# Decode attention at the end of the V stream: a second step multiplied in turned form

## The chip, the cores and the metric

The kernel runs on one core of one Trainium2 chip. The metric is device time in microseconds, some 1.7 us more than the span from the first to the last instruction that a profile shows; runs are quoted as medians with their range.

Engines: PE is the matrix engine (PEld its weight loads), DVE the vector engine, ACT the scalar engine, POOL the general one, SP the queue that issues the big loads. The *granted clock* is the share of PE's full clock that the profile shows as granted, 1.0 or 0.5. A transfer's *landing* is the moment at which the profile shows it complete. The *tail* is what happens from the last softmax to the end.

## The reference

One token attends to a cache of 65536 keys; 16 query heads share 8 heads of K and V, 256 wide. A small token mixer is added through a gate. Only the attention matters here:

```python
Hq, Hkv, Sk, Dh = 16, 8, 65536, 256
scores = einsum("bhqd,bhkd->bhqk", q, k) * (Dh ** -0.5)
p = softmax(scores, axis=-1)
o = einsum("bhqk,bhkd->bhqd", p, v)          # sum over 65536 keys
a = o.reshape(B, Sq, Hq * Dh) @ wo
...                                          # b: the mixer, small
return g * a + (1 - g) * b
```

K and V together are 537 MB in bf16 (2 x 8 x 65536 x 256 x 2 bytes), and each byte is read once. The kernel is a stream.

## The kernel before

Each head's keys are cut into chunks of 5 or 6 steps of 16 key blocks (128 keys each). A chunk's K and V each land in one slot of a ring of three. For every step DVE turns K (`turn`), and PE multiplies it with the queries (`scores`). After the chunk, ACT takes exponentials, DVE turns them (`pT`), and `p_v` multiplies V with them, eight matmuls for a step.

`p_v` keeps the probabilities as weights and streams 512 columns of V through PE. Its result has rows that must be summed and turned onto partitions: `pv` is copied to SBUF (`pvs`), and `o_turn` multiplies it with selector columns, in fp32, into `o_ps`. The *turned form*, `p_v_turned`, does it the other way about: V is the weights, the probabilities are two columns, and the result is added to `o_ps` directly. It takes 32 matmuls of 2 columns for a step in place of 8 of 512, and needs neither copy nor `o_turn`. The kernel before uses it for the very last step alone, which comes as two pieces of 12 and 4 key blocks.

```python
TAIL = 4

def load(item):
    ...
    elif item == 2 * total - 1:              # the last chunk: K and V in pieces
        for s in range(last):
            piece(item - 1, s * SB, SB)      # K, 1 MB each
        for s in range(last - 1):
            piece(item, s * SB, SB)          # V steps 0 to 3, 1 MB each
        piece(item, (last - 1) * SB, SB - TAIL)   # V step 4: 768 KB
        piece(item, last * SB - TAIL, TAIL)       # V step 4: 256 KB

def p_v(i, s):
    ...
    for k in range(SB // 2):
        ...
        nc.tensor.matmul(
            pv[g % 2][32 * a:32 * a + 4, :], lhsT=pT[:, k, :, s], rhs=vt[:, j * DH:(j + 2) * DH], ...)

def o_turn(g):                               # 4 fp32 matmuls (8 in the trace): pvs -> o_ps
    ...
def p_v_turned(i, s, lo, hi):
    ...
    for j in range(lo, hi):
        for c in range(2):
            at = (s * SB + j) * DH + c * 128
            nc.tensor.matmul(
                o_ps[:, 2 * c:2 * c + 2], lhsT=vt[:, at:at + 128], rhs=pT[:, j, :, s], ...)

...                                          # in the loop over chunks, at the end of a chunk:
    for s in range(sizes[c] - (i == total - 1)):
        p_v(i, s)
...                                          # after the loop:
nc.vector.tensor_copy(out=pvs[:, 0:DH], in_=pv[g % 2][:, 0:DH])
nc.scalar.activation(out=pvs[:, DH:2 * DH], in_=pv[g % 2][:, DH:2 * DH], func=ACT.Copy)
o_turn(g)
p_v_turned(i, s, 0, SB - TAIL)
p_v_turned(i, s, SB - TAIL, SB)
...                                          # scale (oT), output projection (acc), bias (res), store
```

The softmax here doesn't subtract the row's maximum and nothing guards it: scores larger than these inputs give would overflow.

## Time and profile before

| | before |
|---|---|
| time | 1273.73 us (1273.19 to 1273.82, 3 runs) |
| span of the profiled run | 1272.2 us |
| busy: PE / DVE / ACT | 57% / 49% / 5% |
| HBM read | 428 GB/s over the span |

The first view is the page's part in 40 slices. DMA is the busy share of the 16 DMA engines in tenths.

```profile
DMA  9999999999999999999999999999999999999997
GB/s 408 426 428 433 432 439 429 429 432 433 435 432 431 431 433 435 431 432 431 432 438 429 432 433 437 435 425 435 431 435 436 427 432 435 436 438 425 432 429 301
```

The stream is full from start to end. The Trainium skill, "DMA: Bandwidth & Descriptors", section "Where 436 GB/s comes from", gives a fabric ceiling of 435 GB/s; all but the first and the last of this trace's slices lie at it (425 to 439). The same section has a lower limit, about 358 GB/s, bind for loads from HBM; this trace of one core read 428, so here the measurement decides. So only what happens after the stream has run dry can be shortened by a change of PE's work. That is the last slice, and the next view shows it: the timeline of the last 10 us. Columns are start, duration, engine, line, operation, result and operands, count, and in brackets the idle time of the engine just before and what ended it.

```profile
1262.25 2.73 PE L382 MATMUL pv<-ring,pT 128*4 128x512 bf16 x24
...
1265.25 0.81 PE L382 MATMUL pv<-ring,pT 128*4 128x512 bf16 x8 [0.26 <-DMA ring<-in_A_v_cache_dram]
...
1266.11 0.42 DVE L472 COPY pvs<-pv 128x256 f32<-128x256 f32 x1 [3.32 <-PE pv L382]
...
1266.59 1.05 PE L414 MATMUL misc<-sel,pvs 128*128 128x2 f32 x8 [0.54 <-DVE pvs L472]
...
1267.51 0.97 PE L425 MATMUL misc<-pT,ring 128*128 128x2 bf16 x32
```

The order: 24 `p_v` for steps 0 to 2, a wait for step 3's V piece, 8 `p_v` for it, the copy, `o_turn` (L414), 32 turned matmuls (L425). The chain of waits names the same things as the ones that decided the end (start, duration, what):

```profile
1245.05 20.16 DMA ring<-in_A_v_cache_dram
1265.20 0.04 issue
1265.25 0.84 PE pv L382 x8
1266.09 0.02 issue
1266.11 0.44 DVE pvs L472
1266.55 0.04 issue
1266.59 1.05 PE misc L414 x8
1267.64 0.84 PE misc L425 x32
```

Two more numbers are needed: when the last pieces land. The view of DMA issues over a window gives the time from issue to landing, in its last column. This is the 256 KB piece, issued at 1249.86:

```profile
ring<-in_A_v_cache_dram SPq DMA_DIRECT2D x1, 256.0 KB, 17.8
```

It lands at 1249.86 + 17.8 = 1267.66. The 768 KB piece lands at 1247.51 + 19.5 = 1267.0. (Landing times are printed to a tenth, so these sums are good to 0.05 us, and a difference of two of them to 0.1.) The last turned matmul ends at 1268.49, which is 0.83 us after the last byte is there.

### The profile page before, as it was taken

The page shows a single profiled execution, that of the slowest core. Times are in us where ns is not written, and L with a number is a line of the kernel's source. Part 1 is how long each engine was busy: PE and PEld are TensorE (multiplying, and loading weights), DVE is VectorE, ACT ScalarE, POOL GpSimd, SP SyncE. Part 2 cuts the span into 40 slices and gives each one's busy share as a digit, 9 for nine tenths or more (in the row PEclk, how much of TensorE's full clock was granted, in tenths as well). Part 3 has the DMA queues.
Part 4 walks back from the last instruction along what each step waited for, and adds up shares of the span by engine and source line. Part 5 has one row for each costly group of instructions (what it writes and reads, how often), then busy time and mean ns, then how long its engine had stood idle before and what let it go on. Part 6 is the DMA issues. An engine that isn't in the chain of part 4 may idle for free.

```text
span 1272.2 us, 10454 instructions
## 1 busy us (share of the span) xinstructions
PE 723.6 (57%) x4552; PEld 285.1 (22%) x4552; DVE 626.8 (49%) x388; ACT 58.4 (5%) x149; POOL 78.5 (6%) x145
## 2 busy tenths in 40 slices
PE   1566556654666546564565646655465555665467
PEld 1222122221222112221222212222122212222123
DVE  2555354644555355453554445544455435544455
ACT  0000000000000000000000000000000000000000
POOL 4110101111011110110000000000000000000000
PEclk9978777888788877888778888888788887878778
DMA  9999999999999999999999999999999999999997
GB/s 408 426 428 433 432 439 429 429 432 433 435 432 431 431 433 435 431 432 431 432 438 429 432 433 437 435 425 435 431 435 436 427 432 435 436 438 425 432 429 301
DMA packets 16842, 544.90 MB, mean 428 GB/s; under 512 B 2202, under 2 KB 2332, under 8 KB 3484
## 3 DMA queue, kind: packets, MB, share of 16 engines
q1 hardware_dynamic: 15416, 540.55, 98.5%
q0 software_dynamic: 1376, 3.69, 0.8%
q8 instruction: 35, 0.57, 0.2%
q14 instruction: 11, 0.09, 0.0%
q10 hardware_dynamic: 4, 0.00, 0.0%
HBM read 544.22 MB, written 0.00 MB: 428 GB/s over the span
## 4 chain that ended last, share of the span: by engine, by line
DMA 63%; PE 17%; DVE 11%; issue 8%; ACT 1%; POOL 0%; DVEq 0%; ACTq 0%; SPq 0%; POOLq 0%
DMA ring<-in_A_k_cache_dram 59%; PE sc L359 12%; DVE kT L351 9%; PE pv L382 5%; DMA zb<-in_B_b_dram 2%; DMA ring<-in_A_v_cache_dram 2%; DVE pT L370 1%; ACT p L366 1%; PE den_ps L398 0%; PE misc L270 0%; DVEq L351 0%; PE acc L314 0%; PE misc L414 0%; PE misc L274 0%; PE misc L425 0%
## 5 line engine op out<-in xcount | busy, mean ns | idle before, releaser
L359 PE MATMUL sc<-kT,qw 128*128 128x512 bf16 x2048 | 575.7, 434 | 443.8 <-DVE kT L351 442.8
L351 DVE STREAM_TRANSPOSE kT<-ring 128x2048 f32<-128x2048 f32 x256 | 575.3, 2288 | 478.1 <-DMA ring<-in_A_k_cache_dram 396.1
L359 PEld LDWEIGHTS <-qw 128*128 128x128 bf16 x2048 | 215.5, 108 | 791.5 <-DVE kT L351 332.2
L382 PE MATMUL pv<-ring,pT 128*4 128x512 bf16 x2040 | 125.7, 395 | 62.1 <-DVE pT L370 61.8
L370 DVE STREAM_TRANSPOSE pT<-p 128x512 bf16<-128x512 bf16 x48 | 34.2, 712 | 130.9 <-ACT p L366 130.9
L382 PEld LDWEIGHTS <-pT 128*4 128x4 bf16 x2040 | 46.6, 89 | 135.0 <-DVE pT L370 81.7
L366 ACT ACTIVATE p<-sc 128x512 bf16<-128x512 f32 x48 | 28.7, 597 | 1037.6 <-PE sc L359 1037.6
L143 POOL DMA_DIRECT2D wo<-in_A_wo_dram x8 | 6.3, 790 | 549.7 <-PE acc L314 549.7
L333 POOL TENSOR_SCALAR t_b<-t_b 128x448 f32<-128x448 f32 x14 | 7.9, 564 | 224.8 <-ACT t_b L325 224.5
L336 POOL TENSOR_TENSOR t_b<-t_b,u_b 128x448 f32<-128x448 f32 x14 | 16.0, 1142 | 1.2
L343 POOL TENSOR_TENSOR gel<-t_b,u_b 128x448 bf16<-128x448 f32 x14 | 15.9, 1133 | 1.2
L339 POOL TENSOR_SCALAR t_b<-t_b,half_g 128x448 f32<-128x448 f32 x14 | 8.9, 636 | 106.9 <-ACT t_b L338 101.9
L414 PEld LDWEIGHTS misc<-sel,pvs 128*128 128x128 f32 x64 | 11.8, 258 | 3.7 <-issue 2.0
L398 PE MATMUL den_ps<-pick,dsum 128*128 128x2 f32 x32 | 4.8, 256 | 12.5 <-DVE dsum L390 12.5
L227 PE MATMUL misc<-zb,one_f 1*128 1x2 f32 x2 | 0.5, 342 | 19.7 <-DMA zb<-in_B_b_dram 19.7
L325 ACT ACTIVATE t_b<-h_bc,b1T,w1T 128x448 f32<-128x448 f32 x14 | 10.5, 751 | 4.7 <-DVE h_bc L257 4.7
L414 PE MATMUL misc<-sel,pvs 128*128 128x2 f32 x64 | 10.2, 281 | 0.5 <-DVE pvs L472 0.5
L329 POOL TENSOR_SCALAR u_b<-h_bc,w1T,b1T 128x448 f32<-128x448 f32 x14 | 10.0, 716 | 2.1 <-DVE qT L277 0.9
L230 DVE TENSOR_SCALAR gate<-gate 128x2 f32<-128x2 f32 x1 | 0.2, 169 | 18.9 <-ACT gate L229 18.9
L366 ACT ACTIVATION_READ_ACCUMULATOR p<-sc 128x1 f32 x48 | 9.3, 194 | 0.0
L164 POOL TENSOR_SCALAR_AFFINE_SELECT pick<-pick 128x2 f32<-128x2 f32 x44 | 8.6, 197 | 3.0 <-POOL pick L164 0.2
L338 ACT ACTIVATE t_b<-t_b 128x448 f32<-128x448 f32 x14 | 8.0, 572 | 13.4 <-POOL t_b L336 13.4
(75 smaller groups left out, 66.0 us busy)
## 6 DMA issues: line engine op xcount, KB each, us to landing
ring<-in_A_k_cache_dram SPq DMA_DIRECT2D x31, 5120.0 KB, 29.8
ring<-in_A_v_cache_dram SPq DMA_DIRECT2D x31, 5120.0 KB, 23.4
ring<-in_A_k_cache_dram SPq DMA_DIRECT2D x16, 6144.0 KB, 33.0
ring<-in_A_v_cache_dram SPq DMA_DIRECT2D x16, 6144.0 KB, 28.0
ring<-in_A_k_cache_dram SPq DMA_DIRECT2D x5, 1024.0 KB, 25.1
ring<-in_A_v_cache_dram SPq DMA_DIRECT2D x4, 1024.0 KB, 22.6
wo<-in_A_wo_dram POOLq DMA_DIRECT2D x8, 448.0 KB, 19.5
ring<-in_A_wq_dram SPq DMA_DIRECT2D x1, 3072.0 KB, 10.1
```

The costliest lines, as they stand in the source:

```text
L164: nc.gpsimd.affine_select(out=t, in_=t, compare_op=ALU.not_equal, fill=1.0, base=-row, pattern=[[step, w]], channel_multiplier=1,)
L325: nc.scalar.activation(out=t_b[:], in_=h_bc[:], func=ACT.Square, scale=w1T[:, b:b + 1], bias=b1T[:, b:b + 1],)
L329: nc.gpsimd.tensor_scalar(out=u_b[:], in0=h_bc[:], scalar1=w1T[:, b:b + 1], scalar2=b1T[:, b:b + 1], op0=ALU.mult, op1=ALU.add,)
L336: nc.gpsimd.tensor_tensor(out=t_b[:], in0=t_b[:], in1=u_b[:], op=ALU.mult)
L339: nc.gpsimd.tensor_scalar(out=t_b[:], in0=t_b[:], scalar1=1.0, scalar2=half_g[:, 0:1], op0=ALU.add, op1=ALU.mult,)
L343: nc.gpsimd.tensor_tensor(out=gel[:], in0=t_b[:], in1=u_b[:], op=ALU.mult)
L351: nc.vector.transpose(out=kT[n % 2][:].bitcast(FP32), in_=kn[:, s * SB * 128:(s + 1) * SB * 128])
L359: nc.tensor.matmul(sc[i % 2][:], lhsT=qw[g % 2][:, q, PAD - s:PAD - s + 128], rhs=kv[:, :, q // 2, :, q % 2], start=(s == 0 and q == 0), s ...
L366: nc.scalar.activation(out=p_t[i % 2][:], in_=sc[i % 2][:], func=ACT.Exp, scale=scale, accum_out=den[g % 2][:, c:c + 1],)
L370: nc.vector.transpose(out=pT_t[i % 2][:], in_=p_t[i % 2][:])
L382: nc.tensor.matmul(pv[g % 2][32 * a:32 * a + 4, :], lhsT=pT[:, k, :, s], rhs=vt[:, j * DH:(j + 2) * DH], start=first and k < 4, stop=last ...
L414: nc.tensor.matmul(o_ps[:, 2 * c:2 * c + 2], lhsT=pvs[:, lo:lo + 128], rhs=sel[:, 2 * half:2 * half + 2], start=(half == 0 and c == 0), st ...
```

## The change

Step 3 is taken from `p_v` and multiplied in turned form too. The intent: the sums of steps 0 to 2 are copied and turned while step 3's V is still on its way, so that after the landing only turned matmuls are left.

```diff
-        last = (g, c, s) == (HKV - 1, n_chunks - 1, sizes[c] - 2)
+        last = (g, c, s) == (HKV - 1, n_chunks - 1, sizes[c] - 3)
@@ p_v_turned
-                    start=False, stop=(j == SB - 1 and c == 1), skip_group_check=True,
+                    start=False, stop=(s == sizes[-1] - 1 and j == SB - 1 and c == 1), skip_group_check=True,
@@ end of a chunk
-        for s in range(sizes[c] - (i == total - 1)):
+        for s in range(sizes[c] - 2 * (i == total - 1)):
             p_v(i, s)
@@ after the loop
     o_turn(g)
+    p_v_turned(i, s - 1, 0, SB)
     p_v_turned(i, s, 0, SB - TAIL)
     p_v_turned(i, s, SB - TAIL, SB)
```

On PE, 8 matmuls of 512 columns go out and 32 of 2 columns come in, after `o_turn` instead of ahead of it. No other engine's order changes.

## The prediction

> **What bounds the kernel.** The stream of K and V out of HBM. The page's DMA row is 9 in 39 of 40 slices, 428 GB/s over the span of 1272.2 us; PE is busy 57%, DVE 49%. The Trainium skill, "DMA: Bandwidth & Descriptors", section "Where 436 GB/s comes from", puts the fabric ceiling at 435 GB/s; this trace's slices (408 to 439 GB/s) sit at it. The change leaves it alone: only the last part of PE's instructions differs. So only the tail counts.
>
> **The tail before** (timeline and chain of waits, us from the span's start). K's last turn ends at 1258.2, scores at 1260.2, softmax and its transpose at 1261.6, den at 1262.25. Then 24 matmuls of p_v for steps 0 to 2 take 2.73 us, without a wait for a DMA, to 1264.98; PE's granted clock is 0.5 from about 1262.3 to 1265.7. Step 3 is waited for 0.26 us: its V piece (issued 1245.05, 20.16 us to landing) lands at 1265.21. The chain from there: 8 matmuls of p_v 0.84, copy of pv 0.44, o_turn 1.05 (weights of the next group start 0.81 after its start), 32 turned matmuls to 1268.49, oT 0.17, acc 0.40, res 0.33, store. The last two pieces (768 and 256 KB) land at 1267.0 and 1267.66, from issue time plus time to landing.
>
> **What changes.** Removed: 8 matmuls of p_v (0.84 us) and the wait (0.26 us) ahead of the copy; copy and o_turn start 1.1 us earlier, at about 1265.0 and 1265.5. Added: 32 turned matmuls; 32 took 0.97 us, 30 ns each, so +0.97 us. These lie on the critical path too, because PE becomes free at about 1266.4, when step 3 has long landed: 64 turned matmuls need 1.94 us, to about 1268.35. Gain: 1.11 - 0.97 = 0.14 us. The floor is the last piece: 1267.66 plus 8 matmuls (0.25 us) and drain, about 1268.0; so 0.5 us is the most that could be gained without moving the stream.
>
> Against it: o_turn now begins at 1265.5, where the clock was still 0.5; 0.2 us or more of it could run at half speed and eat the gain. The Trainium skill, "TensorE: Matmul & The Clock Gate", section "What's actually happening", says that the clock is judged over free-running windows of 3.4 us; the trace agrees (0.5 for 3.4 us). Their phase may differ from run to run.
>
> So PE's work is exchanged nearly one for one. Effect -0.1 us, plausibly -0.5 to +0.6; runs of before differ by 0.6 us.
>
> **Predicted time:** 1273.6 us, 8 in 10 within 1272.2 to 1274.9. Faster by over 2%: 0.5%; within 2%: 99%; slower: 0.5%.
>
> **What would show it.** The timeline: the copy of pv starts before or at the landing of step 3's piece (about 1265.0); o_turn no longer follows a DMA wait; 64 turned matmuls in one run, 1.9 to 2.0 us; end of the last turned matmul to end of span as before (about 3.7 us). In the chain, p_v for the last step's 8 matmuls is gone, and the DMA link ends either at an earlier K piece (the chain then passes through scores, softmax and 24 p_v matmuls) or at one of the last two V pieces.
>
> **What would make it wrong.** A stream that is faster or slower by 0.1% (1.3 us) on this build or chip, which would hide everything. The turned matmuls running at half clock (60 ns each: +2 us). The last pieces landing later.

## The result

| | median us | range | runs |
|---|---|---|---|
| before | 1273.78 | 1273.19 to 1274.00 | 4 |
| after | 1274.62 | 1273.23 to 1275.34 | 4 |
| ratio | 1.0006 | 95%: 0.9989 to 1.0023 | |

Ratios are those on record; they are not quite the ratios of the medians that I quote. The verdict is "same". The profiled run of the changed kernel has a span of 1271.5 us. Its timeline at the end:

```profile
1261.82 1.47 PE L382 MATMUL pv<-ring,pT 128*4 128x512 bf16 x24
...
1263.35 0.42 DVE L472 COPY pvs<-pv 128x256 f32<-128x256 f32 x1 [0.98 <-PE pv L382]
...
1263.83 1.05 PE L414 MATMUL misc<-sel,pvs 128*128 128x2 f32 x8 [0.53 <-DVE pvs L472]
...
1264.75 0.98 PE L425 MATMUL misc<-pT,ring 128*128 128x2 bf16 x32
...
1266.58 0.98 PE L425 MATMUL misc<-pT,ring 128*128 128x2 bf16 x32 [0.85 <-DMA ring<-in_A_v_cache_dram]
```

and its chain of waits:

```profile
1247.59 18.93 DMA ring<-in_A_v_cache_dram
1266.53 0.05 issue
1266.58 0.99 PE misc L425 x32
1267.57 0.02 issue
1267.59 0.17 DVE oT L478
```

The 256 KB piece was issued at 1249.96 in this run:

```profile
ring<-in_A_v_cache_dram SPq DMA_DIRECT2D x1, 256.0 KB, 17.2
```

Three things differ from before. Step 3's `p_v` has left the chain. `p_v` of the other steps took 1.47 us, not 2.73, because the granted clock was 1.0 here and 0.5 in the profile of before. And PE now *waits* 0.85 us, with everything else done, for the 768 KB piece of step 4. The last turned matmul ends at 1267.57, which is 0.41 us after the last landing (1249.96 + 17.2 = 1267.16), where before it was 0.83.

So this one pair of traces would say "0.4 us gained" (0.83 against 0.41), while the runs say "0.8 us lost". Both are below the 0.1% by which single runs differ, and the two traces were not at the same clock. The two profiled runs were also the slowest of the four of before (1274.00) and the fastest of the four of the changed kernel (1273.23). The experiments sort this out.

### The profile page after: what moved, and what is told of

The parts are those of the page before. It is cut to its first block, busy times and chain, and to the rows that moved or that the text cites. A ratio compares the mean times of both kernels' runs of the same rounds, so it can differ in the third digit from the quotient of the medians. Undisturbed runs are those within 1.5% of the kernel's fastest.

```text
span 1271.5 us, 10502 instructions
## 1 busy us (share of the span) xinstructions
PE 740.7 (58%) x4576; PEld 291.7 (23%) x4576; DVE 627.8 (49%) x388; ACT 58.4 (5%) x149; POOL 78.4 (6%) x145
## 4 chain that ended last, share of the span: by engine, by line
DMA 62%; PE 19%; DVE 11%; issue 6%; ACT 1%; POOL 0%; DVEq 0%; ACTq 0%; SPq 0%; POOLq 0%
DMA ring<-in_A_k_cache_dram 59%; PE sc L359 14%; DVE kT L351 9%; PE pv L382 5%; DMA zb<-in_B_b_dram 2%; DMA ring<-in_A_v_cache_dram 1%; DVE pT L370 1%; ACT p L366 1%; PE den_ps L398 0%; PE misc L270 0%; PE acc L314 0%; DVEq L351 0%; PE misc L425 0%; PE misc L274 0%; DVE dsum L390 0%
## 5 line engine op out<-in xcount | busy, mean ns | idle before, releaser
L359 PE MATMUL sc<-kT,qw 128*128 128x512 bf16 x2048 | 587.8, 441 | 425.6 <-DVE kT L351 424.3
L359 PEld LDWEIGHTS <-qw 128*128 128x128 bf16 x2048 | 218.9, 109 | 780.9 <-DVE kT L351 324.0
## 6 DMA issues: line engine op xcount, KB each, us to landing
wo<-in_A_wo_dram POOLq DMA_DIRECT2D x8, 448.0 KB, 18.8
```

What stands on the lines that cost most here:

```text
L359: nc.tensor.matmul(sc[i % 2][:], lhsT=qw[g % 2][:, q, PAD - s:PAD - s + 128], rhs=kv[:, :, q // 2, :, q % 2], start=(s == 0 and q == 0), s ...
```

## The experiments

Two theories at first. **A**: the change shortens the tail by a few tenths, by filling a wait with work, and that is lost in the scatter of the stream. **B**: the change itself costs the 0.06%. As a rival inside A stood the reckoning of the prediction: PE's own chain of work decides, and the exchange 0.84 for 0.97 us settles the gain.

### Both kernels again

No edit. Both were run for five rounds beside common runs of the kernel before.

> The kernel before, unchanged, as the ruler: what two equal kernels differ by. Theory A (the change is worth 0.1 to 0.4 us in the tail, whole runs differ by more): ratio to before 1.000 with single runs spread over 0.5 to 2 us. Tail in the profile: from the landing of the last V piece to the last turned matmul 0.5 to 0.9 us, depending on whether p_v of the tail falls into a half-clock window. Theory B (the change itself costs 0.06%, 0.8 us): this run shows 1.0000 and the run of the changed kernel beside it shows 1.0006 again.

> The changed kernel, unchanged, a second time beside the ruler. Theory A: ratio within 0.999 to 1.001 and not distinguishable from the ruler; in the profile the last turned matmul ends about 0.4 us after the last V piece lands if the clock is full, and up to 0.9 us if p_v runs at half clock (then 64 turned matmuls in one run, no wait). Theory B: 1.0006 again, that is 0.8 us slower, with a later landing of the last V piece.

Measured: the kernel before again 1273.75 us (1273.50 to 1274.22, 5 runs), ratio 1.0000, interval 0.9987 to 1.0012. The changed kernel again 1273.68 us (1273.29 to 1275.07, 5 runs), ratio 1.0001, interval 0.9988 to 1.0015. The shared runs of before were 1273.92 us (1273.23 to 1274.46, 9 runs). The 0.06% did not come back in the medians. The interval still contains 1.0006, so the times alone do not exclude theory B; no trace of this pair shows a tail that the change made longer.

Their traces: both ran the 24 `p_v` at full clock in 1.47 us. Before again ended its turned matmuls 0.71 us after the last landing (1267.83 against 1250.02 + 17.1), the changed kernel 0.43 us (1267.82 against 1250.29 + 17.1). In the trace of before, the wait for step 3's piece had grown to 1.64 us. So the first profile's half clock is not there in every run, and between these two the tail differs by 0.28 us in favour of the change (in the trace of before the clock fell to 0.5 in the last part of `o_turn`).

### Both kernels with the clock held up

Six matmuls of 512 columns, whose result is overwritten, fill the time in which PE waits for the last softmax.

```diff
         softmax(i)
+        if i == total - 1:
+            kf = kT[(n - 1) % 2][:].rearrange("p (j b y two) -> p j b y two", j=SB, b=4, two=2)
+            for _ in range(6):
+                nc.tensor.matmul(
+                    den_ps[:], lhsT=qw[g % 2][:, 0, PAD:PAD + 128], rhs=kf[:, :, 0, :, 0],
+                    start=True, stop=True,
+                )
         if c == n_chunks - 1:
```

> The kernel before with 6 idle-time matmuls (128x512, result overwritten) between the last scores and the denominator, so that PE's clock is full in the whole tail. Theory A: granted clock 1.0 from 1260 us on, 24 p_v matmuls in 1.5 us, the wait for step 3's V piece grows from 0.26 to about 1.4 us, and from that landing to the last turned matmul 2.9 us in place of 3.28; the last turned matmul ends 0.4 to 0.6 us after the last piece lands. Rival (chain of PE work decides, as the prediction had it): the end of the turned matmuls moves with the clock by over 1 us against the landing.

> The changed kernel with the same 6 filler matmuls. Theory A: as in its first profile: the turned matmuls of step 3 finish before the 768 KB piece of step 4 lands, PE waits 0.8 to 1.0 us for it, the last turned matmul ends 0.4 us after the last landing and 1.0 us after the 768 KB piece: at full clock the change gains 0.0 to 0.2 us. Rival (the exchange of PE work decides): no wait between the two groups of 32 turned matmuls, and 0.14 us gained whatever the clock.

Measured in the traces: the granted clock is 1.0 in both until all turned matmuls are done. In the timeline of before with the filler, the 8 `p_v` of step 3 and the turned matmuls:

```profile
1265.44 0.61 PE L382 MATMUL pv<-ring,pT 128*4 128x512 bf16 x8 [1.40 <-DMA ring<-in_A_v_cache_dram]
...
1267.49 0.96 PE L425 MATMUL misc<-pT,ring 128*128 128x2 bf16 x32
```

The timeline of the changed kernel with the filler:

```profile
1265.19 0.97 PE L425 MATMUL misc<-pT,ring 128*128 128x2 bf16 x32
...
1266.87 0.98 PE L425 MATMUL misc<-pT,ring 128*128 128x2 bf16 x32 [0.71 <-DMA ring<-in_A_v_cache_dram]
```

The landings on which the comparison rests: step 3's piece and the 768 KB piece (issued at 1247.65) of before, and the 768 KB piece of the changed kernel:

```profile
1245.20 20.20 DMA ring<-in_A_v_cache_dram
...
ring<-in_A_v_cache_dram SPq DMA_DIRECT2D x1, 768.0 KB, 19.6
...
1247.90 18.92 DMA ring<-in_A_v_cache_dram
```

Before needs 3.07 us from the landing of step 3's piece (1265.40) to the last turned matmul (1268.47), 0.66 us after the last landing. The changed kernel needs 1.04 us from the landing of the 768 KB piece (1266.82), 0.39 us after the last landing. In before with the filler, 1.85 us lie between those two landings (1265.40 and 1247.65 + 19.6), so the gain is 3.07 - 1.85 - 1.04 = 0.18 us counted from the 768 KB piece, or 0.66 - 0.39 = 0.27 us counted from the last one; with the unrounded landing times of the packed traces both come to 0.21. (Expected were 2.9 us and 0.4 to 0.6 us for before, and a wait of 0.8 to 1.0 us for the changed kernel, so the sizes were missed by 0.1 to 0.2 us.) That is theory A, and not the rival: at full clock the landing decides, and not PE's exchange. Times: 1273.51 and 1273.54 us (4 runs each), ratio 0.9998 for both, interval 0.9985 to 1.0012 and 0.9984 to 1.0011. A gain of 0.2 us is 0.016% and cannot be seen in these.

### Both kernels without the wait

If the gain is only a filled wait, it must turn into a loss when there is nothing to wait for. With the filler in place, the last chunk's V pieces but the first are not loaded; PE reads what the slot held, and the result is wrong.

```diff
-            for s in range(last - 1):
+            for s in range(last - 4):
                 piece(item, s * SB, SB)
-            piece(item, (last - 1) * SB, SB - TAIL)
-            piece(item, last * SB - TAIL, TAIL)
```

> The kernel before with the filler matmuls, and without the last four V pieces but one: steps 1 to 4 of the last chunk read what the ring's slot held before (a wrong result on purpose), so no V piece is waited for. PE's chain alone is measured, at full clock. Theory A (the change wins only by filling a wait): 32 p_v matmuls without a break in 1.9 us, then copy and o_turn, then 32 turned; from the first p_v to the end of the last turned matmul 4.3 us.

> The changed kernel in the same way: 24 p_v in 1.5 us, copy and o_turn, then 64 turned in one run. Theory A: from the first p_v to the end of the last turned matmul 4.8 us, that is 0.4 to 0.6 us LONGER than the kernel before with the same edit: without the wait the change costs time, because 32 turned matmuls take 0.97 us and the 8 p_v that they replace 0.43 us at full clock. Rival (the change shortens PE's own chain, as the 0.84 us of p_v in the first profile suggest): shorter or equal.

Measured, timeline of before without the wait:

```profile
1262.10 1.90 PE L380 MATMUL pv<-ring,pT 128*4 128x512 bf16 x32
...
1265.45 0.97 PE L423 MATMUL misc<-pT,ring 128*128 128x2 bf16 x32
```

and of the changed kernel without the wait:

```profile
1262.78 1.47 PE L380 MATMUL pv<-ring,pT 128*4 128x512 bf16 x24
...
1265.69 1.79 PE L423 MATMUL misc<-pT,ring 128*128 128x2 bf16 x64
```

From the first `p_v` to the end of the last turned matmul (by the chain, 1266.43 and 1267.50), before takes 4.33 us and the changed kernel 4.72: 0.39 us longer, just under the 0.4 to 0.6 expected. The terms: 8 `p_v` cost 0.43 us (1.90 - 1.47), and 32 more turned matmuls cost 0.82 (1.79 - 0.97). As work on PE, the turned form is the dearer one; it pays only because it is done while V is still coming.

### Both kernels with PE idle ahead of p_v

This makes the case that the prediction had computed, `p_v` at half clock, which no trace of the changed kernel had shown. The last two steps' scores take 1 matmul of 8 (wrong result), and three copies on ACT keep the softmax at its time.

```diff
-        for q in range(8):
+        few = i == total - 1 and s >= sizes[c] - 2
+        for q in range(1 if few else 8):
...
-                start=(s == 0 and q == 0), stop=(s == sizes[c] - 1 and q == 7),
+                start=(s == 0 and q == 0), stop=(s == sizes[c] - 1 and (few or q == 7)),
...
+        if i == total - 1:
+            for _ in range(3):
+                nc.scalar.activation(out=t_b[:], in_=sc[i % 2][:, 0:D], func=ACT.Copy)
         softmax(i)
```

> The kernel before with PE kept idle ahead of p_v: the last two steps' scores take 1 matmul of 8 (a wrong result on purpose), and three copies on ACT keep softmax at its old time. Theory A: granted clock 0.5 during p_v, 24 p_v in 2.7 us, as in the first profile; the wait for step 3's piece 0.0 to 0.4 us; from that landing to the last turned matmul 3.3 us or more, the last turned matmul 0.8 to 1.0 us after the last landing.

> The changed kernel with the same idle PE: the case that the prediction had computed and that no trace of the changed kernel has shown. Theory A: 24 p_v in 2.7 us, copy of pv at about 1265.0, o_turn from 1265.5, in part at clock 0.5, 64 turned matmuls in one run of 1.9 to 2.1 us, the last ending 0.7 to 1.0 us after the last landing (gain 0.0 to 0.3 us). Rival (the change is limited by the landing of the 768 KB piece whatever the clock): a wait between the two groups of 32 and 0.4 us after the last landing.

Measured, timeline of before with PE idle:

```profile
1263.05 3.33 PE L383 MATMUL pv<-ring,pT 128*4 128x512 bf16 x32
...
1266.91 1.05 PE L415 MATMUL misc<-sel,pvs 128*128 128x2 f32 x8 [0.54 <-DVE pvs L476]
...
1267.83 0.97 PE L426 MATMUL misc<-pT,ring 128*128 128x2 bf16 x32
```

and of the changed kernel with PE idle:

```profile
1262.77 2.73 PE L383 MATMUL pv<-ring,pT 128*4 128x512 bf16 x24
...
1266.04 1.87 PE L415 MATMUL misc<-sel,pvs 128*128 128x2 f32 x8 [0.53 <-DVE pvs L476]
...
1267.77 1.85 PE L426 MATMUL misc<-pT,ring 128*128 128x2 bf16 x64
```

Neither expectation of the changed kernel held. `o_turn` took 1.87 us, all of it at half clock, and the last turned matmul ended 2.03 us after the last landing (1269.63 against 1250.20 + 17.4). Before ended 1.48 us after it (1268.81 against 1250.13 + 17.2), with `o_turn` in 1.05 us; I had expected 0.8 to 1.0. The edit lets `p_v` start late: 4.28 us ahead of the last landing, where it was 5.41 in the first profile of before; 0.4 us of that is that the matmuls for the denominator run at half clock too (1.01 us for 0.61). The change *loses* here: from the first `p_v` to the last turned matmul 6.86 us against 5.76. (After the last landing only 0.55 of these 1.10 us show, because in the look of the changed kernel `p_v` happened to start earlier, 4.8 us ahead of it.)

The reason stands in the granted clock, the number just before the DMA share in the view of windows. Two windows in before with PE idle:

```profile
1266.00:1267.00 1.00, 0.46 (x9) 0.09 (x1) 0.42 (x1) 0.11 (x1) 0.00 (x0) 1.00 0.13 51
1267.00:1268.00 1.00, 1.00 (x15) 1.00 (x16) 0.00 (x0) 0.27 (x1) 0.00 (x0) 1.00 0.00 0
```

and the same in the changed kernel with PE idle:

```profile
1266.00:1267.00 1.00, 0.96 (x5) 0.96 (x5) 0.00 (x0) 0.38 (x1) 0.00 (x0) 0.50 0.16 61
1267.00:1268.00 1.00, 1.00 (x14) 1.00 (x14) 0.00 (x0) 0.00 (x0) 0.00 (x0) 0.50 0.02 6
```

Before is back at full clock when `o_turn` begins, the changed kernel is not, and stays at 0.5 to the end. Was that chance, or do the 8 `p_v` that the change removes keep PE at work long enough for the clock to rise?

### The clock: chance or the missing p_v

Theory **D**: the clock rises only at the end of a window of 3.4 us that was filled with wide matmuls, and 24 `p_v` don't fill one. Rival **E**: chance, the window lay badly. Both cold kernels were repeated without an edit, and in a third 8 `p_v`-shaped matmuls, with a result that nobody reads, were put into the changed kernel's gap between `p_v` and `o_turn`:

```diff
+    pTd = pT_t[i % 2][:].rearrange("p (i b x) -> p i b x", b=4, x=16)
+    for k in range(8):
+        a = k % 4
+        nc.tensor.matmul(
+            pv[(g + 1) % 2][32 * a:32 * a + 4, :], lhsT=pTd[:, k, :, 0],
+            rhs=ring[(2 * i + 1) % RING][:, 2 * k * DH:(2 * k + 2) * DH],
+            start=True, stop=True, tile_position=(0, 32 * a),
+        )
     o_turn(g)
     p_v_turned(i, s - 1, 0, SB)
```

> A repeat of the kernel before with PE idle ahead of p_v, to see whether the first look was a chance of the window's phase. Theory D (the clock rises again only at the end of a window of about 3.4 us that PE streamed for over some 80% of; the 8 p_v that the change removes help to fill it): the clock rises to 1.0 before o_turn, o_turn takes 1.05 us, last turned matmul 0.8 to 1.6 us after the last landing. Rival E (chance): o_turn at half clock, 1.9 us.

> A repeat of the changed kernel with PE idle ahead of p_v. Theory D: with 24 p_v (2.56 us at half clock, 75% of a window at most) the clock stays at 0.5 in o_turn and in the turned matmuls: o_turn 1.87 us, the last turned matmul about 2 us after the last landing, later than in the kernel before with the same edit. Rival E: at another phase the clock rises and o_turn takes 1.05 us.

> The changed kernel with PE idle ahead of p_v, and 8 p_v-shaped matmuls into the bank of the other head put back between p_v and o_turn (result unused). Theory D: PE streams 3.4 us as in the kernel before, the clock rises to 1.0 during or just after it, o_turn takes 1.05 to 1.5 us in place of 1.87, and the last turned matmul ends 0.3 to 0.8 us earlier after the first p_v than the 6.9 us without the fill, although PE has 0.85 us more work. Rival E: o_turn 1.87 us, the end 0.3 us later than without the fill.

Measured: the repeats did as the first looks. Before: `o_turn` 1.05 us, 5.83 us from the first `p_v` to the end. Changed: `o_turn` 1.87 us, 6.86 us. With the fill, in the timeline:

```profile
1262.83 2.73 PE L383 MATMUL pv<-ring,pT 128*4 128x512 bf16 x24
...
1265.35 0.69 PE L481 MATMUL pv<-ring,pT 128*4 128x512 bf16 x8
...
1266.10 1.05 PE L415 MATMUL misc<-sel,pvs 128*128 128x2 f32 x8
...
1267.01 1.80 PE L426 MATMUL misc<-pT,ring 128*128 128x2 bf16 x64
```

`o_turn` is back at 1.05 us, and the whole takes 6.00 us in place of 6.86, although PE does 8 matmuls more. That is what theory D says. It is one trace, though, and of the fill only 0.15 us, 4% of a window, lay ahead of the window's end. The moment at which each trace's clock fell can be read from the windows, and decisions come in steps of 3.41 us from there (1262.29 and 1265.70 in the first profile of before). Counting how long `p_v` streamed in the step that held most of it (an estimate: 0.427 us for four matmuls at half clock, by their spacing in the timeline): the clock rose after 90% (before cold again), 88% (before), 86% (before cold) and, with the fill, 79% of the window, and didn't after 75% and 63% (the two looks of the changed kernel with PE idle), though PE counted as busy all through the window with 75%. The 24 `p_v` come to 6 x 0.427 = 2.56 us, 75% of a window at the best.

All windows of the 14 traces, up to the last change of the clock in each, can be counted in the same way, in steps of 3.41 us from each change. This is an estimate too: wide matmuls, those of 512 columns, stream for 0.427 us at half clock and 0.216 at full clock by their spacing, and four `p_v` that run side by side count once. Of 1782 windows at half clock, none of the 1022 with under 69% of wide work was followed by a rise, all 682 with 77% or more were, and of the 78 between, 14. Of 3254 windows at full clock, all 706 with under 35% were followed by a fall, and none of the 2543 with over 36%. So rival E falls, in that the clock follows the wide work in the window; where the windows lie still decides how much that is. The 24 `p_v` are at the edge both ways: 75% at half clock, and 38% (6 x 0.216 us) at full clock.

### One step more in turned form

> The changed kernel with the filler matmuls at full clock and one step more turned (16 p_v left, 96 turned). Theory A (at full clock the tail hangs on the landing of the 768 KB piece, and work moved ahead of it is worth nothing): PE still waits for that piece, 0.3 to 1.0 us, the last turned matmul ends 1.05 us after it and 0.4 us after the last landing, as with two steps turned; time within 0.1% of before. Rival (each turned step saves as much again): 0.1 us or less after the last landing.

The edit is the change once more, on the changed kernel with the filler: `p_v` for steps 0 and 1, turned form for 2, 3 and 4. Measured: 1273.72 us (1273.41 to 1273.77, 4 runs), ratio 0.9999, interval 0.9982 to 1.0015. In the timeline:

```profile
1265.40 2.70 PE L425 MATMUL misc<-pT,ring 128*128 128x2 bf16 x96
```

The 96 turned matmuls ran without a break in 2.70 us, so the expected wait of 0.3 to 1.0 us was not there; in this run the first `p_v` stood only 4.09 us ahead of the 768 KB piece's landing (1262.91 against 1248.20 + 18.8), where it was 4.55 in the run with two steps (1262.27 against 1266.82), and the additional work took up the slack. The last turned matmul ended 1.12 us after the 768 KB piece and 0.45 us after the last landing, as good as with two steps. So the third step gains nothing and leaves no slack. Nor was the clock full to the end, as the expectation had it: with 16 `p_v` left it fell to 0.5 at 1266.32, amid the turned matmuls.

No version beat both kernels clear of the scatter.

## Why the prediction was right, and where its steps failed

**The time and the class were right.** "1273.6 us, 8 in 10 within 1272.2 to 1274.9" holds both medians of the changed kernel, 1274.62 and 1273.68. Its main step was that the stream bounds the kernel, that the change leaves it alone, and that at most 0.5 us of tail could be won; the traces show 0.2 to 0.3 us won at full clock. That step was reasoned. That the small gain came out near 0.14 us was luck: neither term of the sum 1.11 - 0.97 decided the end at full clock. The range of 2.7 us would have been met by any tail half a microsecond shorter or longer.

**"PE becomes free at about 1266.4, when step 3 has long landed: 64 turned matmuls need 1.94 us" failed at full clock.** The prediction took the first profile's `p_v` of 2.73 us as a property of the kernel. It was one of two cases: in all three looks at full clock (the two of the changed kernel and one with the filler) PE waited 0.57 to 0.85 us between two groups of 32. The gain was mis-sized: 0.14 us as an exchange of PE work, 0.18 to 0.27 us measured at the same clock as a wait that is filled. The floor, "1267.66 plus 8 matmuls (0.25 us) and drain, about 1268.0", 0.35 us after the last landing, was met nearly: 0.39 to 0.43.

**"PE's work is exchanged nearly one for one" fails at full clock.** The prediction counted 0.84 us out and 0.97 in. At full clock it is 0.43 for 0.82, as the pair without the wait shows, and alone it makes the tail 0.39 us longer. At half clock it would be about 0.85 for 0.9 (an estimate: 2 x 0.427 us, and half of the 1.85 us of 64 turned matmuls); no pair of runs isolates it there.

**"0.2 us or more of it could run at half speed and eat the gain" was the right risk with the wrong size.** The prediction kept the moment at which the clock rises, 1265.7, from the trace of before. But that rise was earned by the 8 `p_v` that the change removes. Where `p_v` runs at half clock, all of `o_turn` does: 1.87 us in place of 1.05, and the changed kernel ended later after the last landing by 0.55 and 0.58 us in the two pairs of looks (2.03 and 2.25 us against 1.48 and 1.67).

**"The turned matmuls running at half clock (60 ns each: +2 us)" was wrong.** At clock 0.5, 64 took 1.85 us, 29 ns each; at 1.0, 1.79 us.

**What the zero is made of.** The change wins 0.2 to 0.3 us where the clock is up and loses over half a microsecond in the cases made with PE idle. Both are below the scatter. What stays open is how often the half clock comes by itself: of the four plain looks, one of before had it in `p_v`, none of the changed kernel. Three of the 9 runs of the changed kernel took over 1274.9 us, while none of the 26 plain runs of before (the two equal kernels together) took over 1274.46, and none of the 12 runs with the filler over 1273.94. That would fit a tail at half clock, but those slow ones were not traced, so it is argued and not shown. The only two plain looks at the changed kernel were at its fastest run of four and of five, and the mean granted clock of the three slow runs (0.831 to 0.835) lies among those of the others (0.812 to 0.841). A half-clock tail would be common enough: between the last scores and `p_v` PE does no wide work for some 2.25 us (from about 1260.0, when the last score matmul has streamed, to 1262.25 in the first profile), so a window that holds this whole gap has at most 1.16 us of wide work, 34%, and by the count above is followed by a fall. By the windows' position alone that would meet about a third of all runs (an estimate: 1.16 of 3.41), and the filler, which closes the gap, would prevent it. Theory B is left in this form, as a change that now and then costs a microsecond; the mean of the 9 runs is 1274.11 us, that of the 26 plain runs of before 1273.80.

## What to carry to other kernels

A kernel bound by a stream has a tail that can be optimised to the tenth of a microsecond without the measured time showing it; measure from the last landing, not from the start, and ask first whether the gain exceeds the scatter. Moving work ahead of a landing is worth the wait that it fills, even where the work itself becomes dearer, and nothing once the landing decides. A single profile shows one state of the matrix engine's clock: before costing a change from it, ask what keeps that clock up and whether the change removes it.

## What the Trainium skill lacked or had wrong

- "TensorE: Matmul & The Clock Gate", section "What's actually happening": it states free-running windows of about 3.4 us and two rates. The traces agree (0.5 from 1262.29 to 1265.70; only 0.5 and 1.0 were granted). It says that the array is warm after one busy window, but not what share of a window makes it busy: here a window with PE busy throughout, 75% of it wide `p_v` matmuls, didn't raise the clock, 79% did; and the window after it, busy for 2.88 of 3.41 us with almost only fp32 and 2-column matmuls, didn't either. In the count over all traces the clock always rose from 77% of wide work on and never under 69%, and at full clock fell under 35% and held over 36%.
- The same page, section "Wait — 56ns, not 53.3ns?", has a floor of about 25 ns between small matmuls. The traces agree: about 26 ns from start to start for turned matmuls with their weight loads (64 in 1.79 us, of which the last one takes 0.165). The page gives its example at full clock and doesn't say that such a stream is nearly the same at half clock: about 27 ns (64 in 1.85 us).
- The same page, section "Weight-path perf modes — Fast Weight Load (FWL) and DoubleRow", says that the fast load of 128 weights is used for types other than FP32. That would fit what is seen, but no run here isolates it. The page doesn't say how a weight load's time goes with the granted clock: the fp32 `o_turn` goes from 1.05 to 1.87 us with the clock (its weight loads from 192 to 333 ns), and the bf16 turned matmuls' weight loads only go from 96 to 103 ns.
- "DMA: Bandwidth & Descriptors" has nothing on how the DMA engines' busy share goes at the end of a stream. Here it falls to about 0.5 some 5 us before the last landing (225 GB/s from 1261.9 to 1263.2 in the changed kernel's profile, 149 from 1263.8 to 1266.4), with all pieces issued 17 us or more ahead. Why, these traces don't show.
